# A quarter of w2's last row in twenty-four partitions: an adaLN decode block on one core

## The chip, the cores and the metric

One NeuronCore of a Trainium2 chip runs the whole kernel. The metric is the device time of one execution in microseconds; the median of the runs counts. The engines are called as in the profile: PE is TensorE's matmuls and PEld its weight loads, DVE is VectorE, ACT is ScalarE, POOL is GpSimd, SP is SyncE, which issues nearly all DMAs. A name with a q behind it (SPq, PEq) is the sequencer of that engine.

## What is computed

Two tokens (B = 2, one position each) go through a block with adaptive layer norm. The conditioning vector gives six modulation vectors. Attention runs over the last 4,096 positions of a cache with 8 key-value heads, and a dense feed-forward with SiLU follows. All is float32.

```python
mod = (_silu(c) @ w_mod).reshape(c.shape[0], 6, 1, -1)
sa, ca, ga, sb, cb, gb = (mod[:, 0], mod[:, 1], mod[:, 2], mod[:, 3], mod[:, 4], mod[:, 5])
h = _layernorm(x, axis=-1) * (1 + ca) + sa
x = x + ga * _A_ref(h, A_k_cache, A_v_cache, A_wq, A_wo)   # q = h@wq, softmax(q k) v, @wo
h = _layernorm(x, axis=-1) * (1 + cb) + sb
x = x + gb * _B_ref(h, B_w1, B_w2)                         # silu(h @ w1) @ w2
```

The sizes: D = 512, 32 query heads of 128, F = 1792; w2 has 1,792 rows of 512 columns.

## The kernel before

**The stream.** Every large input passes once through a ring of eight slots of 128 partitions x 16 KB (`slots`, handed out by `stream`). SP issues the loads in the order in which they are written: w_mod, wq, then for each of eight steps a pair of heads of K and of V (`load_pair`, L82, 4 MB each, two slots), wo in two loads, w1 in two, w2 in four (`load_runs`, L93). A load waits until the slots that it takes are free, and so SP runs some loads ahead of the compute. The step's loads are issued in `fetch(s)` (L351): K of step s, then V of step s - 1; `fetch(s + 1)` is called at the beginning of step s.

**The steps.** In step s, DVE transposes K in 32 x 32 blocks (`keys`, L363), PE multiplies it with the queries (`scores`, L376), DVE and ACT build the softmax, and PE multiplies the weights of the step before with V (`weighted`, L450). The queries stand in two constant tiles, `qbd[0]` for the first four heads and `qbd[1]` for the other four (`place`, L316). `scores` of steps 0 to 3 reads `qbd[0]` and that of steps 4 to 7 reads `qbd[1]`.

**How a weight is laid out.** A weight of 1,792 rows is read as 128 partitions of 14 rows, "(p t) e -> p t e": partition p holds rows 14 p to 14 p + 13, and `tile tt` is row tt of every partition, [128, 512]. The hidden vector is brought into the same layout: `uT` [128, 14, 32] holds in column 0 and 16 of its last axis the two tokens, and zeros between them.

**The last product.** w2's four loads are rows 0 to 7 of each partition (2 MB), 8 to 10 (768 KB), 11 and 12 (512 KB), and 13 (256 KB). Each matmul takes a [128, 32] slice of `uT` as weights and writes 32 output rows, chosen by g:

- L663, tiles 0 to 7: the full 512 columns each; tile tt writes rows 32 (tt mod 4) and up of `yw`. `gather` (L548) copies yw to SBUF (L551 on ACT, L552 on DVE) and adds it up into `y` by four matmuls (L554).
- L673, tiles 8 to 10: four matmuls for a tile, g = 0 to 3, 128 columns each, into `y`.
- L688, tiles 11 to 13: for each half h of 64 columns of a block of 128, and for g = 0 to 3, one matmul, into `yl[0]` or `yl[1]`. The last load feeds tile 13, eight of these 24 matmuls.

DVE then forms yp = y * gb + x1 (L696, L697), yo = yl * gb for each half (L701), yo + yp for each half (L704), and SP writes yo out (L706).

**What sets the order.** Instructions wrapped in `inorder` keep their written order on their engine; the others are placed by a scheduler by when their inputs are ready (the copy of L505 stands behind the loop in the code and runs at 31.5 us, before it). `busy(n)` issues n matmuls on data that nobody reads, each into the same 32 rows of `junk` (L567).

Of the kernel before, what the change touches and what calls it, by code (L numbers as in the profile page):

```python
# [10 lines left out]
ALU = mybir.AluOpType  # L11
AX = mybir.AxisListType

P = 128
B, D = 2, 512
HQ, HKV, DH = 32, 8, 128
G = HQ // HKV
F = 1792
EPS = 1e-5
RING = 8  # L20


@with_exitstack
def adaln_block(
# [19 lines left out]
    nc = tc.nc  # L44
# [16 lines left out]
    def const(shape, name):  # L61
        return consts.tile(shape, F32, name=name)

    def bank(tag, name):
        return (psum1 if tag in "CO" else psum).tile([P, 512], F32, tag=tag, name=name)


    slots, turn_of = ring.tile([P, RING, 4096], F32, name="slots"), [0]

    def stream(n=1):  # L70
        i = turn_of[0]
        if n % 2 == 0:
            i += -i % n
        turn_of[0] = i + n
        return slots[:, i % RING : i % RING + n, :].rearrange("p s e -> p (s e)")

    def load_pair(cache, s):


        i, b = divmod(s, B)  # L80
        t = stream(2)
        nc.sync.dma_start(  # L82
            t,
            cache[b, 2 * i : 2 * i + 2, SK - W :, :].rearrange("e (u n) d -> u e (n d)", u=P // 2),
        )
        return t

    def load_runs(w, per, lo, hi):

        e = w.shape[1]  # L90
        n = -(-(hi - lo) * e // 4096)
        t = stream(n)[:, : (hi - lo) * e].rearrange("p (q e) -> p q e", e=e)
        nc.sync.dma_start(t, w.rearrange("(p q) e -> p q e", q=per)[:, lo:hi, :])  # L93
        return t
# [5 lines left out]
    ident = const([P, P], "ident")  # L100
# [6 lines left out]
    for b in range(B):  # L107
# [53 lines left out]
    odd = const([P, 2], "odd")  # L161
    nc.vector.tensor_reduce(
        odd, ident.rearrange("p (a r) -> p r a", r=2), axis=AX.X, op=ALU.add
    )

    selg0, selg = const([P, G], "selg0"), const([P, B, G], "selg")
# [42 lines left out]
    qbd = [const([P, 4, B, 4, 32], f"qbd{n}") for n in range(2)]  # L209
# [11 lines left out]
    def silu_exp(t, name, shape):  # L221

        e = once.tile(shape, F32, tag="silu", name=name)
        nc.vector.tensor_scalar(e, t, -1.0, 87.0, op0=ALU.mult, op1=ALU.min)
        nc.scalar.activation(e, e, AF.Exp)
        nc.vector.tensor_scalar(e, e, 1.0, None, op0=ALU.add)
        nc.vector.reciprocal(e, e)
        return e
# [26 lines left out]
    def turned(t, name):  # L255
        o = const([P, 4, 32], name)
        nc.vector.transpose(o, t.rearrange("p (m k) -> p k m", k=4))  # L257
        return o
# [7 lines left out]
    for k in range(4):  # L266
        ab = wm[:, k, : 2 * D].rearrange("p (s g m) -> p g s m", s=2, g=4)
        cd = wm[:, k, 2 * D :].rearrange("p (s g m) -> p g s m", s=4, g=4)
        for g in range(4):
            r = slice(32 * g, 32 * g + 32)  # L270
            nc.tensor.matmul(m_a[r, :], scT[:, k, :], ab[:, g], start=(k == 0), stop=(k == 3))  # L271
        for g in range(4):
            r = slice(32 * g, 32 * g + 32)
# [19 lines left out]
    hT, uT = const([P, 4, 32], "hT_b"), const([P, F // P, 32], "uT")  # L293
# [6 lines left out]
    for n in range(2):  # L300
        for k in range(4):
            wv = wqt[:, k, :].rearrange("p (n s g m) -> p n g s m", n=2, s=4, g=G)
            for g in range(G):
# [4 lines left out]
                    start=(k == 0),  # L308
                    stop=(k == 3),
                )  # L310

    inorder = tc.keep_in_program_order
# [32 lines left out]


    STEPS = B * HKV // 2
    kt, vt, wot, kT = {}, {}, [], {}
    s_ps, pr, o_ps, o_sb = {}, {}, {}, {}

    def fetch(s):  # L351

        if s < STEPS:
            kt[s] = load_pair(k_cache, s)
        if s > 0:
            vt[s - 1] = load_pair(v_cache, s - 1)

    def keys(s, j):


        kT[s, j] = ktp.tile([P, 64, 32], F32, tag="kT", name=f"kT{s}_{j}")
        for c in range(2):
            inorder(nc.vector.transpose(  # L363
                kT[s, j][:, 32 * c : 32 * c + 32, :],
                kt[s].rearrange("p (n j r) -> p j n r", j=4, r=32)[:, j, 32 * c : 32 * c + 32, :],
            ))

    def scores(s, j):

        if j == 0:  # L370
            s_ps[s] = bank("A", f"s{s}")
        i, b = divmod(s, B)
        for c in range(2):
            for e in range(2):
                r, h = 64 * e + 32 * c, 2 * i + e
                inorder(nc.tensor.matmul(  # L376
                    s_ps[s][r : r + 32, :],
                    qbd[h // 4][:, h % 4, b, j, :],
                    kT[s, j][:, 32 * c : 32 * c + 32, e:32:2],
                    start=(j == 0),  # L380
                    stop=(j == 3),
                ))
# [34 lines left out]
    def turn(s):  # L417

        xp = once.tile([P, 16, 32], F32, tag="xp", name=f"xp{s}")
        inorder(nc.vector.transpose(xp, pr[s]))  # L420
        zp = once.tile([P, 4, 16, 16], F32, tag="zp", name=f"zp{s}")
        inorder(nc.vector.tensor_mul(  # L422
            zp,
            xp[:, None, :, 0:16].to_broadcast([P, 4, 16, 16]),
            quarter[:, :, None, None].to_broadcast([P, 4, 16, 16]),
        ))
        tp = bank("C", f"pT{s}")[:, : 2 * P]
        for i in range(4):
            inorder(nc.tensor.matmul(  # L429
                tp[32 * i : 32 * i + 32, :],  # L430
                mix.rearrange("p v e -> p (v e)"),
                zp.rearrange("p y t x -> p (y t) x")[:, :, 4 * i : 4 * i + 4],
                start=True,
                stop=True,
            ))
        for e in range(2):
            inorder(nc.scalar.activation(  # L437
                ptb[s % 2][:, :, e, :],
                tp.rearrange("p (w z) -> p w z", z=16),
                AF.Copy,  # L440
                scale=odd[:, e : e + 1],
            ))
# [19 lines left out]
    def collect(s):  # L462
# [3 lines left out]
        for m in range(4):  # L466
# [5 lines left out]
                start=(s == 0 and m < 2),  # L472
                stop=(s == STEPS - 1 and m >= 2),
                skip_group_check=True,
            ))

    fetch(0)
    keys(0, 0)
    for s in range(STEPS + 1):
        if s < STEPS:  # L480
            fetch(s + 1)
            scores(s, 0)
        if s > 0 and s != STEPS - 1:
            turn(s - 1)
        if s > 1:
            collect(s - 2)
        if s == 2:
            place(1)
        if s < STEPS:
            for j in range(1, 4):  # L490
# [15 lines left out]
    ax = once.tile([P, P], F32, tag="ax", name="ax")  # L506
    for lo, hi in ((0, 24), (24, 32)):
        wt = load_runs(wo, 32, lo, hi)
        wot.extend(wt[:, q, :] for q in range(hi - lo))
    xT = turned(x_sp, "xT")  # L510
    w1t = []
    for lo, hi in ((0, 3), (3, 4)):
# [11 lines left out]
    for r in (0, 64):  # L524
# [4 lines left out]
            start=True,  # L529
            stop=True,  # L530
# [33 lines left out]
    def busy(n):  # L564

        for _ in range(n):
            inorder(nc.tensor.matmul(  # L567
                junk[0:32, :],
                id4,
                quad.rearrange("p m y -> p (m y)"),  # L570
                start=True,
                stop=True,
            ))
# [5 lines left out]
    for q in range(28):  # L579
        g = q % 4  # L580
# [4 lines left out]
            start=(q < 4),  # L585
            stop=(q >= 24),
        ))
    for q in range(28, 32):
        for g in range(4):
# [4 lines left out]
                start=(q == 28),  # L594
                stop=False,
            ))
    gather(ao, acc, "acc_o_sb", False, True)
    busy(1)
    T2, WIDE = F // P, 8
    w2t = {}  # L600
    for lo, hi in ((0, WIDE), (WIDE, 11), (11, 13), (13, T2)):
        wt = load_runs(w2, T2, lo, hi)
        for tt in range(lo, hi):
            w2t[tt] = wt[:, tt - lo, :]
    aoT = once.tile([P, 4, 32], F32, tag="zp", name="aoT")
    nc.vector.transpose(aoT, ao.rearrange("p (m k) -> p k m", k=4))
    x1T = once.tile([P, 4, B], F32, tag="x1T", name="x1T")
# [19 lines left out]
    for k in range(4):  # L627
        for g in range(4):
# [4 lines left out]
                start=(k == 0),  # L633
                stop=(k == 3),
# [22 lines left out]
        )  # L657
    sg = silu_exp(z, "sgh", [P, T2, B])
    nc.vector.tensor_mul(uT[:, :, 0:32:16], z, sg)
    yw = bank("D", "acc_yw")  # L660
    for tt in range(WIDE):
        g = tt % 4
        inorder(nc.tensor.matmul(  # L663
            yw[32 * g : 32 * g + 32, :],
            uT[:, tt, :],
            w2t[tt],
            start=(tt < 4),
            stop=(tt >= WIDE - 4),
        ))
    y = bank("D", "acc_y")[:, :P]  # L670
    for tt in range(WIDE, 11):
        for g in range(4):
# [4 lines left out]
                start=(tt == WIDE),  # L677
                stop=False,
# [2 lines left out]

    H = P // 2
    yl = [bank("A", f"acc_l{h}")[:, :H] for h in range(2)]
    for tt in range(11, T2):
        for h in range(2):
            for g in range(4):
                lo = g * P + h * H
                inorder(nc.tensor.matmul(  # L688
                    yl[h][32 * g : 32 * g + 32, :],
                    uT[:, tt, :],  # L690
                    w2t[tt][:, lo : lo + H],
                    start=(tt == 11),
                    stop=(tt == T2 - 1),
                ))
    yp = once.tile([P, P], F32, tag="xp", name="yp")
    inorder(nc.vector.tensor_mul(yp, y, gb))  # L696
    inorder(nc.vector.tensor_add(yp, yp, x1))  # L697
# [1 line left out]
    for h in range(2):  # L699
        r = slice(h * H, (h + 1) * H)  # L700
        inorder(nc.vector.tensor_mul(yo[:, r], yl[h], gb[:, r]))  # L701
    for h in range(2):
        r = slice(h * H, (h + 1) * H)
# [30 lines left out]
```

## Time and profile before

| | |
|---|---|
| median of 3 runs | 235.45 us (235.43 to 235.75) |
| span of the profiled execution, first to last instruction | 233.7 us |
| busy in it: PE / PEld / DVE / ACT / POOL | 160.2 / 43.1 / 115.6 / 28.5 / 10.6 us |
| mean granted clock of PE | 0.934 of full speed, 1.00 from 190 us on |
| DMA | 3,795 packets, 97.68 MB |
| chain that ended last | DMA 60%, issue 17%, DVE 14%, PE 6% of the span |

The page of the profile gives busy times over the whole span; the chain of waits follows back what released each step, and the timeline lists instructions with their start in us, their length, and in brackets how long the engine had been idle before them and what ended that. x16 means sixteen instructions merged into one line. fp32 matmuls appear as two passes, so eight matmuls are x16. The length of a matmul is modelled and includes its way through the array; starts are as recorded.

### The profile page before, as it was taken

To read this page: it belongs to the slowest core of one execution; us is meant where nothing else is said; L and a number is where in the kernel's file an instruction comes from. 1 tells how busy PE (TensorE), PEld (TensorE's weight loads), DVE (VectorE), ACT (ScalarE), POOL (GpSimd) and SP (SyncE) were. 2 spreads that over 40 slices of the span, in tenths; PEclk is the share of its full clock that TensorE was granted. 3 is DMA by queue.
4 is the path that set the end of the run, shared out by engine and by line. 5 is a ranking of instruction groups with operands and counts; after the bars stand their busy time and mean duration, and the time that the engine had idled before them with its cause. 6 is when DMAs were issued, how large, how long until landed. Compare 5 with 4: busy or idle time off the path is not lost.

```text
span 233.7 us, 2571 instructions
## 1 busy us (share of the span) xinstructions
PE 160.2 (69%) x1070; PEld 43.1 (18%) x1070; DVE 115.6 (49%) x179; ACT 28.5 (12%) x64; POOL 10.6 (5%) x35
## 2 busy tenths in 40 slices
PE   0005916959577839787689759758769777869784
PEld 0001401211111111221111202201112122314223
DVE  3004140178795758696197189249559540101232
ACT  1100210000311120120210201111030031002020
POOL 8600010000000000000000000000000000000000
PEclk9999975879979997999979988999997999999999
DMA  7998998999999999999999999999999999989991
GB/s 269 446 520 381 426 471 359 440 443 428 415 421 449 440 443 421 421 423 449 443 437 426 415 429 449 437 437 429 404 444 443 437 423 471 446 362 427 423 412 57
DMA packets 3795, 97.68 MB, mean 418 GB/s; under 512 B 433, under 2 KB 457, under 8 KB 969
## 3 DMA queue, kind: packets, MB, share of 16 engines
q1 hardware_dynamic: 3768, 97.53, 97.2%
q8 instruction: 8, 0.13, 0.2%
q14 instruction: 3, 0.02, 0.0%
q10 hardware_dynamic: 16, 0.00, 0.0%
HBM read 97.53 MB, written 0.00 MB: 417 GB/s over the span
## 4 chain that ended last, share of the span: by engine, by line
DMA 60%; issue 17%; DVE 14%; PE 6%; POOL 1%; POOLq 0%; SPq 0%; ACT 0%; DVEq 0%
DMA slots<-in_A_k_cache_dram 22%; DMA slots<-in_A_wq_dram 14%; DMA slots<-in_B_w_dram 12%; DMA slots<-in_A_v_cache_dram 12%; DVE kT L363 11%; PE q L304 3%; PE o L450 2%; DVE zp L422 1%; PE acc_yw L663 1%; DVE xp L420 1%; PE acc_y L673 0%; DVE xc L102 0%; POOL qg L321 0%; DVE qT L317 0%; PE acc_y L554 0%
## 5 line engine op out<-in xcount | busy, mean ns | idle before, releaser
L363 DVE STREAM_TRANSPOSE kT<-slots 128x1024 f32<-128x1024 f32 x64 | 73.7, 1210 | 22.9 <-DMA slots<-in_A_k_cache_dram 22.8
L376 PE MATMUL s<-kT,qbd 128*32 128x512 f32 x256 | 68.5, 703 | 17.9 <-DVE kT L363 17.0
L450 PE MATMUL o<-slots,ptb 128*32 128x512 f32 x256 | 29.1, 595 | 2.2 <-DMA slots<-in_A_v_cache_dram 2.2
L376 PEld LDWEIGHTS s<-kT,qbd 128*32 128x32 f32 x256 | 9.8, 113 | 66.9 <-DVE kT L363 62.9
L271 PE MATMUL m_a<-slots,scT 128*32 128x256 f32 x32 | 4.4, 507 | 20.4 <-DVE scT L263 20.4
L304 PE MATMUL q<-slots,hq_T 128*32 128x512 f32 x64 | 9.7, 773 | 7.4 <-DMA slots<-in_A_wq_dram 7.4
L450 PEld LDWEIGHTS o<-slots,ptb 128*32 128x32 f32 x256 | 7.7, 109 | 16.7 <-issue 16.6
L406 ACT COPY bias<-bp 128x1 f32<-128x1 f32 x8 | 1.3, 159 | 75.8 <-PE bp L404 75.8
L386 DVE TENSOR_REDUCE mx<-s 128x1 f32<-128x512 f32 x8 | 5.5, 691 | 9.6 <-PE s L376 9.6
L567 PE MATMUL junk<-quad,id 128*32 128x512 f32 x22 | 10.2, 596 | 0.0
L437 ACT ACTIVATE ptb<-pT,odd 128x256 f32<-128x256 f32 x16 | 6.7, 472 | 26.0 <-PE pT L429 26.0
L422 DVE TENSOR_TENSOR zp<-xp,quarter 128x1024 f32<-128x1024 f32 x8 | 9.8, 1225 | 0.2
L429 PE MATMUL pT<-zp,mix 128*32 128x256 f32 x64 | 5.8, 438 | 4.0 <-DVE zp L422 4.0
L317 DVE STREAM_TRANSPOSE qT<-q 128x512 f32<-128x512 f32 x2 | 1.4, 717 | 13.5 <-PE q L304 12.0
L581 PE MATMUL acc_o<-slots,oTn 128*32 128x512 f32 x56 | 6.2, 593 | 2.3 <-DMA slots<-in_A_wo_dram 2.3
L460 ACT COPY ob<-o 128x512 f32<-128x512 f32 x8 | 4.7, 586 | 24.4 <-PE o L450 24.4
L552 DVE COPY acc_o_sb<-acc_o 128x256 f32<-128x256 f32 x1 | 0.4, 425 | 14.1 <-ACT acc_o_sb L551 14.1
L388 PE MATMUL mT<-ident,mx 128*1 128x128 f32 x16 | 3.0, 270 | 6.3 <-DVE mx L386 6.3
L420 DVE STREAM_TRANSPOSE xp<-pr 128x512 f32<-128x512 f32 x8 | 5.5, 685 | 3.4 <-ACT pr L408 3.4
L257 DVE STREAM_TRANSPOSE cT<-xc 128x128 f32<-128x128 f32 x1 | 0.4, 401 | 13.7 <-DMA xc<-in_c_dram 13.7
L274 PE MATMUL m_sp<-slots,scT 128*32 128x512 f32 x32 | 7.2, 730 | 0.0
L468 PE MATMUL o_all<-ob,selh 128*64 128x128 f32 x64 | 5.9, 313 | 0.8 <-ACT ob L460 0.8
(140 smaller groups left out, 93.7 us busy)
## 6 DMA issues: line engine op xcount, KB each, us to landing
slots<-in_A_k_cache_dram SPq DMA_DIRECT2D x8, 4096.0 KB, 27.6
slots<-in_A_v_cache_dram SPq DMA_DIRECT2D x8, 4096.0 KB, 27.7
slots<-in_w_mod_dram SPq DMA_DIRECT2D x1, 6144.0 KB, 17.2
slots<-in_A_wo_dram SPq DMA_DIRECT2D x1, 6144.0 KB
slots<-in_B_w_dram SPq DMA_DIRECT2D x1, 2688.0 KB
slots<-in_A_wo_dram SPq DMA_DIRECT2D x1, 2048.0 KB, 29.5
slots<-in_B_w_dram SPq DMA_DIRECT2D x1, 2048.0 KB
slots<-in_B_w_dram SPq DMA_DIRECT2D x1, 896.0 KB
```

The lines of the kernel that those rows point to most:

```text
L274: nc.tensor.matmul(m_sp[r, :], scT[:, k, :], cd[:, g], start=(k == 0), stop=(k == 3))
L304: nc.tensor.matmul(q_ps[n][32 * g : 32 * g + 32, :], hq_T[:, k, :], wv[:, n, g], start=(k == 0), stop=(k == 3),)
L363: inorder(nc.vector.transpose(kT[s, j][:, 32 * c : 32 * c + 32, :], kt[s].rearrange("p (n j r) -> p j n r", j=4, r=32)[:, j, 32 * c : 32 * ...
L376: inorder(nc.tensor.matmul(s_ps[s][r : r + 32, :], qbd[h // 4][:, h % 4, b, j, :], kT[s, j][:, 32 * c : 32 * c + 32, e:32:2], start=(j == ...
L420: inorder(nc.vector.transpose(xp, pr[s]))
L422: inorder(nc.vector.tensor_mul(zp, xp[:, None, :, 0:16].to_broadcast([P, 4, 16, 16]), quarter[:, :, None, None].to_broadcast([P, 4, 16, 16 ...
L429: inorder(nc.tensor.matmul(tp[32 * i : 32 * i + 32, :], mix.rearrange("p v e -> p (v e)"), zp.rearrange("p y t x -> p (y t) x")[:, :, 4 * ...
L437: inorder(nc.scalar.activation(ptb[s % 2][:, :, e, :], tp.rearrange("p (w z) -> p w z", z=16), AF.Copy, scale=odd[:, e : e + 1],))
L450: inorder(nc.tensor.matmul(o_ps[s][r : r + 32, :], ptb[s % 2][:, w].rearrange("p e z -> p (e z)"), vt[s].rearrange("p (c w m f d) -> p c f ...
L468: inorder(nc.tensor.matmul(o_all[r : r + 64, :], selh[:, m, lo : lo + 2 * HQ], o_sb[s][:, m * DH : (m + 1) * DH], start=(s == 0 and m < 2) ...
L567: inorder(nc.tensor.matmul(junk[0:32, :], id4, quad.rearrange("p m y -> p (m y)"), start=True, stop=True,))
L581: inorder(nc.tensor.matmul(acc[32 * g : 32 * g + 32, :], oTn[:, q, :], wot[q], start=(q < 4), stop=(q >= 24),))
```

## The change

Of tile 13 of w2 (row 13 of each partition) the columns 384 to 511, those of g = 3, are no longer loaded with the rest for partitions 8 to 127. These 120 pieces of 128 columns go to 24 partitions, five side by side in each (`far` [48, 5, 128], rows 0 to 11 and 32 to 43), inside the memory of `qbd[0]`. Eight loads (`move`) of 3 x 5 pieces bring them: in the order of issue behind V of step 4, K of 6, V of 5, K of 7, V of 6 and V of 7, and one behind each of the two loads of wo. Partitions 0 to 7 (`own` = 8) get their 128 columns by a load of their own, and the other 384 columns of the row come for all partitions in one load.

The hidden values of those 120 partitions must stand in the same 24 partitions. `uj` multiplies tile 13 of `uT` with `slot`, which marks at which of the five places a partition's piece stands; the matmul `up` with the selection matrix `away` sends them to the 24 rows; a copy puts them into `uF` [48, 5, 32], zeroed before. In L688's place the columns of g = 3 are then made by six matmuls for each half: five of 48 rows with `uF` and `far`, one of 8 rows with `uT` and `own`'s columns. They stand between tile 12 and the matmuls of g = 0 to 2 of tile 13.

```diff
+NE, NR, NJ = 3, 4, 5
...
+    own = P - 2 * NR * NJ * NE
+    away, slot = const([P, 48], "away"), const([P, NJ], "slot")
+    nc.gpsimd.memset(away, 0.0)
+    for h in range(2):
+        nc.vector.tensor_reduce(
+            away[:, 32 * h : 32 * h + NE * NR].rearrange("p (e r) -> p e r", e=NE),
+            ident[:, own + 60 * h : own + 60 * h + 60].rearrange(
+                "p (r j e) -> p e r j", r=NR, j=NJ
+            ),
+            axis=AX.X,
+            op=ALU.add,
+        )
+    nc.vector.tensor_reduce(
+        slot,
+        ident[:, own:].rearrange("p (hr j e) -> p j hr e", j=NJ, e=NE),
+        axis=AX.XY,
+        op=ALU.add,
+    )
...
+    T2, WIDE = F // P, 8
+    w2p = w2.rearrange("(p t) e -> p t e", t=T2)
+    spare = qbd[0].rearrange("p s b j c -> p (s b j c)")
+    far = spare[:, : NJ * P].rearrange("p (j m) -> p j m", j=NJ)
+    uF = spare[:, NJ * P : NJ * (P + 32)].rearrange("p (j n) -> p j n", j=NJ)
+    uj = spare[:, NJ * (P + 32) : NJ * (P + 32 + B)].rearrange("p (j b) -> p j b", j=NJ)
+    moves = [(h, r) for h in range(2) for r in range(NR)]
+
+    def move():
+
+        h, r = moves.pop(0)
+        lo = own + 60 * h + NJ * NE * r
+        nc.sync.dma_start(
+            far[32 * h : 32 * h + NE * NR].rearrange("(e r) j m -> e r j m", r=NR)[:, r],
+            w2p[lo : lo + NJ * NE, T2 - 1, D - P :].rearrange("(j e) m -> e j m", e=NE),
+        )
...
             kt[s] = load_pair(k_cache, s)
+            if s > STEPS // 2 + 1:
+                move()
         if s > 0:
             vt[s - 1] = load_pair(v_cache, s - 1)
+            if s > STEPS // 2:
+                move()
...
         wt = load_runs(wo, 32, lo, hi)
+        move()
         wot.extend(wt[:, q, :] for q in range(hi - lo))
+    nc.gpsimd.memset(uF, 0.0)
...
-    for lo, hi in ((0, WIDE), (WIDE, 11), (11, 13), (13, T2)):
+    for lo, hi in ((0, WIDE), (WIDE, 11), (11, 13)):
...
+    w2l = stream(1)[:, :D]
+    nc.sync.dma_start(w2l[0:own, D - P :], w2p[0:own, T2 - 1, D - P :])
+    nc.sync.dma_start(w2l[:, : D - P], w2p[:, T2 - 1, : D - P])
...
     nc.vector.tensor_mul(uT[:, :, 0:32:16], z, sg)
+    nc.vector.tensor_mul(
+        uj,
+        uT[:, T2 - 1, 0:32:16][:, None, :].to_broadcast([P, NJ, B]),
+        slot[:, :, None].to_broadcast([P, NJ, B]),
+    )
     yw = bank("D", "acc_yw")
...
+    up = bank("C", "up")[:48, : NJ * B]
+    inorder(nc.tensor.matmul(
+        up, away, uj.rearrange("p j b -> p (j b)"), start=True, stop=True
+    ))
+    nc.vector.tensor_copy(uF[:48, :, 0:32:16], up.rearrange("p (j b) -> p j b", b=B))
     y = bank("D", "acc_y")[:, :P]
...
-    for tt in range(11, T2):
+    def last(h, g, lhs, rhs, start=False, stop=False):
+        inorder(nc.tensor.matmul(
+            yl[h][32 * g : 32 * g + 32, :], lhs, rhs, start=start, stop=stop
+        ))
+
+    for tt in range(11, T2 - 1):
         for h in range(2):
             for g in range(4):
                 lo = g * P + h * H
-                inorder(nc.tensor.matmul(
-                    yl[h][32 * g : 32 * g + 32, :],
-                    uT[:, tt, :],
-                    w2t[tt][:, lo : lo + H],
-                    start=(tt == 11),
-                    stop=(tt == T2 - 1),
-                ))
+                last(h, g, uT[:, tt, :], w2t[tt][:, lo : lo + H], start=(tt == 11))
+    for h in range(2):
+        for j in range(NJ):
+            last(h, 3, uF[:48, j, :], far[:48, j, h * H : h * H + H])
+        last(
+            h, 3, uT[0:own, T2 - 1, :], w2l[0:own, 3 * P + h * H : 3 * P + h * H + H], stop=True
+        )
+    for h in range(2):
+        for g in range(3):
+            lo = g * P + h * H
+            last(h, g, uT[:, T2 - 1, :], w2l[:, lo : lo + H], stop=True)
```

More of the change, by code (lines that the diff above doesn't have):

```diff
@@ L598, in adaln_block @@
     busy(1)
-    T2, WIDE = F // P, 8
     w2t = {}
-    for lo, hi in ((0, WIDE), (WIDE, 11), (11, 13), (13, T2)):
+    for lo, hi in ((0, WIDE), (WIDE, 11), (11, 13)):
         wt = load_runs(w2, T2, lo, hi)
```

## The prediction

> **What bounds the kernel now.** I read the page first, then the chain of waits that ended last, then the last three microseconds of the timeline.
>
> ```profile
> span 233.7 us, 2571 instructions
> DMA  7998998999999999999999999999999999989991
> DMA packets 3795, 97.68 MB, mean 418 GB/s; under 512 B 433, under 2 KB 457, under 8 KB 969
> ```
>
> The DMA engines are full from the second of the 40 slices to the last but one: the kernel streams 97.68 MB at 418 GB/s, 26 GB/s for each of 16 engines. What can be gained in the stream is what the last bytes cost; what can be lost is anything behind them. The end of the chain, in order of time (start, duration):
>
> ```profile
> 197.41 28.93 DMA slots<-in_B_w_dram
> 226.34 0.14 issue
> 226.47 1.92 PE acc_yw L663 x16
> 228.40 0.78 PE acc_y L673 x24
> 229.18 0.20 PE acc_y L554 x4
> ...
> 229.39 0.44 PE acc_y L554 x4
> ...
> 229.85 0.30 DVE yp L696
> ...
> 230.18 0.29 DVE yp L697
> 230.47 0.35 DVE yo L701 x2
> 230.82 0.13 DVE yo L704
> ```
>
> The end hangs on the first of the four loads of w2 (rows 0 to 7 of a partition, landed at 226.34), not on the last one. From there PE and DVE work through to yo. The change shortens the last load alone, so I look at where that one stands. The first two rows are DMA issues (KB each, us from issue to landing), the third is the line that issues, the fourth is from the timeline:
>
> ```profile
> slots<-in_A_k_cache_dram SPq DMA_DIRECT2D x8, 4096.0 KB, 27.6
> slots<-in_B_w_dram SPq DMA_DIRECT2D x1, 256.0 KB, 17.3
> L93 SPq DMA_DIRECT2D slots<-in_B_w_dram x6: 328/328/328, 190.2 to 212.7; - x6
> 229.54 0.97 PE L688 MATMUL acc_l<-slots,uT 128*32 128x64 f32 x47
> L688 PE MATMUL acc_l<-slots,uT x48: 216/219/243, 229.5 to 230.3; 128*32 128x64 f32 x48
> ```
>
> Issued at 212.7, the last load lands 17.3 later, at 230.0. L688 works off tiles 11, 12 and 13 with 16 matmuls each (8 in the code, two passes for each). They start (0.97 - 0.219) / 46 = 0.016 us apart, so tile 13's turn comes at 229.54 + 32 x 0.016 = 230.05: PE arrives just as the load lands. And L701 starts at 230.47, when L697 is done, so DVE's own chain ends with them. Three things tie: an earlier landing alone can bring no more than about 0.05 us.
>
> **The transfers.** 120 partitions give up 512 of the 2,048 bytes of their last row. Its 128 rows are eight for each of 16 engines, so it loses 4 KB on each, at 26 GB/s 0.16 us. By the tie above 0.05 of it can count, and only if PE is ready then. The 61 KB come back as 120 pieces behind eight earlier loads. The load's outer size is 3; if three engines carry it all, each takes 40 pieces, 20 KB, at 26 GB/s 0.79 us at least. Whether that shows depends on the engines' lead (stretch, length, busy time of PE, PEld, DVE, ACT, POOL, clock, DMA share, GB/s):
>
> ```profile
> 226.00:227.00 1.00, 0.53 (x8) 0.28 (x12) 0.00 (x0) 0.00 (x0) 0.00 (x0) 1.00 1.03 430
> 228.25:228.50 0.25, 0.25 (x12) 0.21 (x12) 0.00 (x0) 0.00 (x0) 0.00 (x0) 1.00 0.54 221
> 228.75:229.00 0.25, 0.25 (x17) 0.23 (x11) 0.09 (x1) 0.13 (x1) 0.00 (x0) 1.00 0.49 188
> 229.50:229.75 0.25, 0.25 (x17) 0.25 (x19) 0.00 (x0) 0.00 (x0) 0.00 (x0) 1.00 0.05 16
> q8 instruction: 8, 0.13, 0.2%
> ```
>
> All engines work at 226 to 227; from 228.25 half of them do; at 229.5 none. So half have a lead of about 1.2 us. The instruction row is one likely reason: 8 packets of 16 KB took 0.2% of 16 engines' 233.7 us, some 0.9 us each, on one engine at a time. If the three engines are of the early half, 0.79 us vanishes in the lead: cost 0 here, and +0.3 to +0.8 otherwise (rival B). The Trainium skill, page "DMA: Bandwidth & Descriptors", section "Why a DMA increments its semaphore by 16 and not by 1", says that such a load is split over the largest number of engines up to 16 that divides both outer sizes, and takes the lowest-numbered: three here. No row shows engine numbers; were the pieces spread over all 16, the sum would be the same, as the landing does not count.
>
> **SP, POOL and DVE.** These rows price what is added and show its cover:
>
> ```profile
> L82 SPq DMA_DIRECT2D slots<-in_A_k_cache_dram x8: 534/534/605, 28.7 to 146.6; - x8
> SPq L82 <- DVE kT L363: 76.8, 7, 13.7
> 17.78 0.40 DVE L257 STREAM_TRANSPOSE cT<-xc 128x128 f32<-128x128 f32 x1 [13.68 <-DMA xc<-in_c_dram]
> 30.69 0.53 POOL L289 TENSOR_SCALAR mod_sp<-mod_sp 128x128 f32<-128x128 f32 x1 [21.22 <-ACT mod_sp L288]
> L162 DVE TENSOR_REDUCE odd<-ident 128x2 f32<-128x128 f32 x1 | 0.3, 274 | 0.0
> 228.91 0.42 DVE L552 COPY acc_y_sb<-acc_yw 128x256 f32<-128x256 f32 x1 [3.39 <-ACT acc_y_sb L551]
> ```
>
> Nine more issues on SP (eight moves, and the last load becomes two) cost about 0.53 each; SP sits waiting for 76.8 us on DVE alone, and a K load issued 27.6 us ahead of its landing needs 4 MB / 418 GB/s = 10.0 us of the stream, so 0.5 us later is nothing. The moves write into qbd[0], last read by step 3's scores; the load ahead of the first move (V of step 4) already waits for step 2's L450, which stands behind those scores on PE. Even if each move had to wait for the piece before it to land, the next load would be issued about one load (10 us) ahead of its turn instead of two or three. The reductions for away and slot (three of 0.27) fall into DVE's idle 13.68 us ahead of L257, the memsets into POOL's 21.22. The product uj falls into DVE's 3.39 ahead of L552. Without these covers they would cost some 0.3 us apiece. All cost 0.
>
> **The matmul `up` and the copy of uF.** `up` goes between L663 and L673. There is a row for such an insertion, L638 within L629:
>
> ```profile
> 219.43 1.71 PE L629 MATMUL hid<-slots,hT_b 128*32 128x448 f32 x16 [0.94 <-DMA slots<-in_B_w_dram]
> 221.07 0.38 PE L638 MATMUL var_b<-vs,mean 128*128 128x2 f32 x2
> 221.39 1.71 PE L629 MATMUL hid<-slots,hT_b 128*32 128x448 f32 x16
> 221.79 0.13 PEld L629 LDWEIGHTS hid<-slots,hT_b 128*32 128x32 f32 x4 [0.25 <-issue]
> 222.16 0.13 PEld L629 LDWEIGHTS hid<-slots,hT_b 128*32 128x32 f32 x4 [0.25 <-issue]
> L638 PE MATMUL var_b<-vs,mean 128*128 128x2 f32 x2 | 0.4, 262 | 0.0
> ```
>
> A round of four L629 matmuls takes 222.16 - 221.79 = 0.37, so the second sixteen would start at 219.43 + 4 x 0.37 = 220.91; they start at 221.39. The insertion cost 0.48: 0.38 - 0.26 = 0.12 between its two passes, and 0.36 for two changes of the array's shape (128*32 to 128*128 and back), 0.18 each. `up` costs PE at most that. L673 then ends late, but the second half of L554 starts at 229.39, only when DVE's L552 (228.91 + 0.42) is done. So about 0.2 us of it are covered, and the copy of uF fits ahead of 228.91 if `up` is done by 228.7. I take +0.05, between 0 and +0.3.
>
> **The matmuls of the moved columns.** Tile 13's two matmuls for g = 3 become twelve (five pieces and `own`, for two halves), 24 passes, all into the same 32 output rows. Today g runs through four row groups. What rotation is worth is in two more rows:
>
> ```profile
> L567 PE MATMUL junk<-quad,id 128*32 128x512 f32 x12 | 5.3, 594 | 0.0
> L541 PE MATMUL oq<-on,quad 128*128 128x64 f32 x8 | 1.1, 277 | 0.8 <-DVE on L538 0.8
> ```
>
> L567 writes one row group over and over: (5.3 - 0.594) / 11 = 0.43 for 512 columns. L663, of the same shape, rotates: 1.92 us for 16, some 0.1 each. So one group is four times slower than four; for 64 columns 0.43 / 8 = 0.054. Bounds: 0.016, L688's rotating pace, and (1.1 - 0.277) / 7 = 0.118 of L541, 64 columns into one output with four times wider weights. I take 0.054, the same width of weights and one group: 24 x 0.054 = **1.30 us**, and nothing hides it, since PE reaches it at 230.05 with all else done. It also falls behind the landing, whose gain is thereby lost.
>
> These matmuls differ in rows too: 128 (tile 12), 48 (pieces), 8 (own), 48, 8, and 128 again for g = 0 to 2: five changes of shape. A change cost 0.18 at L638, there with weights four times as wide; no row shows one of rows alone. Bounds 0 and 0.18, I take 0.12: **+0.60**. The Trainium skill, "TensorEngine Tiling (Array Packing)", section "Key Properties", says that a change of tiling mode drains the engine, while different tiles run in parallel; the L638 row agrees. By that rule all five count, and without it the sum would be 0.60 less.
>
> Removed: four passes at 0.016 and PE's small wait, together 0.1; 0.05 is DVE's slack. **Sum**: 1.30 + 0.60 + 0.05 - 0.10 - 0.05 = +1.80. The profiled execution spans 233.7, and the median of the runs, 235.45, is 1.75 above that, which the change does not touch; so 235.45 + 1.80 = 237.25, **237.2 us**. Both unknown prices at their bounds, one at a time: pace 0.016 gives 236.3 and 0.118 gives 238.8; changes of shape at 0 and 0.18 give 236.6 and 237.5.
>
> **The rivals.** A, not slower: the pieces stream abreast. If PE issues the twelve as fast as the rotating ones and a change of rows alone drains nothing, 24 x 0.016 = 0.38, less 0.15, plus 0.05: +0.3, 235.7. It decides under 0.023 a matmul, where the sum falls under 0.2%. For it: L688's own pace; against it: L567. B, an engine of the late half: one of the three lags; then every load from step 5 on, w2's first too, lands up to 0.8 later. From the lag inside the late half I take +0.5 on top: 237.7. For it: half of the engines are late. C, the wide price: the twelve run at L541's pace, 238.8; its weights speak against it. D, SP: a move holds a load back until the stream runs dry. Against it stands the lead of 10 us: only a wait as long as SP's longest on DVE, 13.7, would use it up, and the stream would stand for 3.7 us: 240.9.
>
> **How the numbers follow.** Forecast 0.60, A 0.06, B 0.20, C 0.08, D 0.03; 0.03 is left, 0.02 of it for a gain that I do not see. The likeliest case alone reaches from 236.6 to 237.5. The range, 236.1 to 238.8, takes in the bounds of the two prices, B and C, and leaves out A and D. Under 0.2% (0.47 us) a measurement here can't be told from no change: faster 0.02, within 0.2% 0.06, slower 0.92.
>
> **What would show it.** In the changed profile: L663's wait ends at 226.3 as before (B: later); the last load lands some 0.1 to 0.2 earlier; the g = 3 matmuls begin near 230.1 and take about 1.9 us with gaps at each change of rows; DVE waits for PE ahead of L701, where today it waits for nothing. If L701 starts before 230.9, or the chain ends in a DMA, the prediction is wrong.

## The result and the profile after

The changed kernel takes 237.94 us (median of 4 runs, 237.79 to 238.09), the kernel before beside it 235.60 (235.43 to 235.76): a ratio of 1.0099, 95% interval 1.0085 to 1.0113, or 2.34 us more. The profiled execution of the changed kernel is the one of 237.79 us. Its page:

```profile
span 235.6 us, 2638 instructions
DMA packets 3955, 97.69 MB, mean 415 GB/s; under 512 B 464, under 2 KB 744, under 8 KB 1128
```

There are 160 packets more, as many bytes as before, and the span is 1.9 us longer. The lines have moved: L663 is now L713, L673 is L728, L554 is L597, L688 is L740, L696 and L697 are L760 and L761, L701 is L765, L704 is L768; `up` is L721. The chain that ended last in the changed kernel (start, duration), in order of time:

```profile
198.98 27.28 DMA slots<-in_B_w_dram
226.26 0.14 issue
226.39 1.92 PE acc_yw L713 x16
228.32 0.19 PE up L721 x2
228.50 0.79 PE acc_y L728 x24
229.30 0.38 PE acc_y L597 x7
229.68 2.57 PE acc_l L740 x61
232.24 0.02 issue
232.27 0.36 DVE yo L765 x2
```

It starts with the same load, which landed at 226.26 (226.34 before), and the first 3.3 us have hardly changed. But it no longer runs over to DVE's yp: PE stays in it with L740 until 232.24, and yo starts at 232.27, 1.80 later than before (230.47). The timeline shows what PE does there (start, length, form of the instructions, and in brackets what DVE waited for):

```profile
228.25 0.26 PE L721 MATMUL up<-qbd,away 128*48 128x10 f32 x2
229.46 0.71 PE L740 MATMUL acc_l<-slots,uT 128*32 128x64 f32 x32
229.78 0.29 DVE L760 TENSOR_TENSOR yp<-acc_y,mod_sp 128x128 f32<-128x128 f32 x1 [0.52 <-PE acc_y L597]
230.10 0.74 PE L740 MATMUL acc_l<-qbd 48*32 48x64 f32 x10
230.78 0.29 PE L740 MATMUL acc_l<-slots,uT 8*32 8x64 f32 x2
231.00 0.74 PE L740 MATMUL acc_l<-qbd 48*32 48x64 f32 x10
231.67 0.65 PE L740 MATMUL acc_l<-slots,uT 8*32 8x64 f32 x14
232.27 0.36 DVE L765 TENSOR_TENSOR yo<-acc_l,mod_sp 128x64 f32<-128x64 f32 x2 [1.87 <-PE acc_l L740]
```

The view of L740 alone has the min, median and max ns of one of these matmuls:

```profile
L740 PE MATMUL acc_l<-qbd x20: 216/216/240, 230.1 to 231.5; 48*32 48x64 f32 x20
```

Tiles 11 and 12 are the 32 passes at 229.46, at 0.016 each. The moved columns begin at 230.10. The ten passes on pieces take 0.74 us and the last of them 0.216, so their starts lie (0.74 - 0.216) / 9 = 0.058 apart on average; in the trace it is 0.056, with one step of 0.080 behind the change of shape ahead of them. From 230.10 to 231.00 lie twelve passes and two changes of shape: 0.90 - 12 x 0.056 = 0.23, or **0.11 for a change**. The merged group at 231.67 is `own`'s two passes and the twelve of g = 0 to 2. DVE, which waited for nothing ahead of L701 before, now waits 1.87 us for PE.

The last load in the changed kernel's timeline of SP, and its row among the DMA issues (KB, us to landing):

```profile
213.82 0.36 SPq L649 DMA_DIRECT2D slots<-in_B_w_dram  x1
```

```profile
slots<-in_B_w_dram SPq DMA_DIRECT2D x1, 192.0 KB, 16.0
```

It lands at 213.82 + 16.0 = 229.8, 0.2 earlier than before, and nobody waits for it. The windows of the changed kernel, in the columns of the prediction:

```profile
228.25:228.50 0.25, 0.25 (x10) 0.23 (x10) 0.00 (x0) 0.07 (x1) 0.00 (x0) 1.00 0.70 279
228.75:229.00 0.25, 0.25 (x17) 0.25 (x12) 0.19 (x2) 0.05 (x1) 0.00 (x0) 1.00 0.52 193
229.50:229.75 0.25, 0.25 (x24) 0.25 (x23) 0.00 (x0) 0.00 (x0) 0.00 (x0) 1.00 0.00 0
```

At 228.25 a share of 0.70 of the DMA engines still works, against 0.54 before: (0.70 - 0.54) x 16 = 2.6, some three engines more. By 228.75 the share is back near a half.

The trace also keeps the times at which a DMA raises the semaphore of a load: sixteen times when a load of 128 partitions lands, read here as once for each engine, and three times when a move lands. For w2's first load in the kernel before, eight of the sixteen come within 0.56 us of the first, and the other eight 1.38 to 2.03 us behind it. In the changed kernel five come within 0.27 us, three 1.16 to 1.28 behind the first, and eight 1.54 to 1.89. So three engines that used to be done early carry the moves and lose about 1 us by them, and they still end ahead of the late ones.

### The profile page after: what moved, and what is told of

Read it like the earlier page. It is cut to its first block, busy times and chain, and to the rows that moved or that the text cites. A ratio compares the mean times of both kernels' runs of the same rounds, so it can differ in the third digit from the quotient of the medians.

```text
span 235.6 us, 2638 instructions
## 1 busy us (share of the span) xinstructions
PE 164.4 (70%) x1092; PEld 44.7 (19%) x1092; DVE 116.4 (49%) x184; ACT 28.5 (12%) x64; POOL 10.8 (5%) x37
## 4 chain that ended last, share of the span: by engine, by line
DMA 60%; PE 18%; DVE 17%; ACT 2%; issue 1%; ACTq 0%; POOL 0%; DVEq 0%; POOLq 0%
DMA slots<-in_A_k_cache_dram 43%; DVE kT L404 12%; DMA slots<-in_B_w_dram 12%; PE s L417 7%; DMA xc<-in_c_dram 6%; PE o L491 4%; PE m_sp L294 2%; DVE zp L463 2%; DVE xp L461 1%; PE acc_l L740 1%; PE m_a L291 1%; PE acc_yw L713 1%; ACT pr L449 1%; DVE mx L427 1%; ACT L449 1%
## 5 line engine op out<-in xcount | busy, mean ns | idle before, releaser
L417 PE MATMUL s<-kT,qbd 128*32 128x512 f32 x256 | 69.6, 684 | 18.7 <-DVE kT L404 17.5
L491 PE MATMUL o<-slots,ptb 128*32 128x512 f32 x256 | 30.5, 619 | 0.1
L324 PE MATMUL q<-slots,hq_T 128*32 128x512 f32 x64 | 9.1, 731 | 7.8 <-DMA slots<-in_A_wq_dram 7.8
L610 PE MATMUL junk<-quad,id 128*32 128x512 f32 x22 | 11.6, 666 | 0.0
L624 PE MATMUL acc_o<-slots,oTn 128*32 128x512 f32 x56 | 7.0, 593 | 0.0
L294 PE MATMUL m_sp<-slots,scT 128*32 128x512 f32 x32 | 6.6, 712 | 0.0
```

Of the source, the lines that this page charges most:

```text
L294: nc.tensor.matmul(m_sp[r, :], scT[:, k, :], cd[:, g], start=(k == 0), stop=(k == 3))
L324: nc.tensor.matmul(q_ps[n][32 * g : 32 * g + 32, :], hq_T[:, k, :], wv[:, n, g], start=(k == 0), stop=(k == 3),)
L417: inorder(nc.tensor.matmul(s_ps[s][r : r + 32, :], qbd[h // 4][:, h % 4, b, j, :], kT[s, j][:, 32 * c : 32 * c + 32, e:32:2], start=(j == ...
L491: inorder(nc.tensor.matmul(o_ps[s][r : r + 32, :], ptb[s % 2][:, w].rearrange("p e z -> p (e z)"), vt[s].rearrange("p (c w m f d) -> p c f ...
L610: inorder(nc.tensor.matmul(junk[0:32, :], id4, quad.rearrange("p m y -> p (m y)"), start=True, stop=True,))
L624: inorder(nc.tensor.matmul(acc[32 * g : 32 * g + 32, :], oTn[:, q, :], wot[q], start=(q < 4), stop=(q >= 24),))
```

## The experiments

All times are medians, each beside runs of the kernel before on the same chip. "Outside" is the median of a run's time less its span. "Tail" is, in the profiled execution, the time from the first matmul on w2 (L663, now L713) to the start of yo (L701, now L765); it leaves out when w2 landed. For the changed kernel it is 232.27 - 226.39 = 5.88.

| kernel | time, us | against before, 95% interval | median span | outside | tail |
|---|---|---|---|---|---|
| before (beside the first four) | 235.53 | | 233.7 | 1.79 | 4.00 |
| the change | 237.94 | 1.0085 to 1.0113 | 235.9 | 2.12 | 5.88 |
| moves and `up`, old tail | 235.75 | 1.0002 to 1.0020 | 233.6 | 2.14 | 4.00 |
| no moves | 237.70 | 1.0082 to 1.0110 | 235.65 | 2.05 | 5.87 |
| all rows | 237.07 | 1.0055 to 1.0083 | 235.0 | 2.10 | 5.21 |
| rotated | 237.11 | 1.0056 to 1.0083 | 235.05 | 2.04 | 5.20 |
| rotated, all rows | 236.19 | 1.0017 to 1.0040 | 234.1 | 2.08 | 4.33 |
| every move twice, old tail | 236.74 | 1.0037 to 1.0066 | 234.7 | 2.05 | 4.04 |
| constants alone | 235.67 | 0.9990 to 1.0009 | 233.8 | 1.81 | 4.00 |

**The old tail with everything else kept.** The moves, `uj`, `up` and the copy of uF stay; the last load and its matmuls are those of before.

```diff
-    for lo, hi in ((0, WIDE), (WIDE, 11), (11, 13)):
+    for lo, hi in ((0, WIDE), (WIDE, 11), (11, 13), (13, T2)):
...
-    for tt in range(11, T2 - 1):
+    for tt in range(11, T2):
...
-    for h in range(2):
-        for j in range(NJ):
-            last(h, 3, uF[:48, j, :], far[:48, j, h * H : h * H + H])
...
```

> The eight moves, the matmul up and the copy of uF stay, but the last load and the last matmuls are those of before (all 128 columns of g = 3 come with the last load; the moved pieces are loaded and not read). Theory, the cost is PE's serial tail alone: within 0.1 us of before, the first load of w2 lands at 226.3 +- 0.1, DVE is again free of PE ahead of yo. Rival, the small loads or the three engines cost it: +1 us or more, with the first load of w2 landing that much later.

235.75 against 235.53. The end of its chain:

```profile
226.58 1.92 PE acc_yw L710 x16
228.51 0.19 PE up L718 x2
...
230.29 0.29 DVE yp L749
230.58 0.35 DVE yo L753 x2
```

The tail is 230.58 - 226.58 = 4.00, that of before to the hundredth, and the span (233.6 in the median) is no longer than before (233.7). `up` takes 0.19 in the chain and costs nothing at its end, as DVE's yp sets it. So the eight moves, their issues, `up` and the copy cost nothing inside the span; what is left, 0.2 us, lies outside it (below).

**The change without its moves.** No `move()`; a memset zeroes `far`, so the moved pieces' share is missing from the result.

```diff
-            if s > STEPS // 2 + 1:
-                move()
...
-            if s > STEPS // 2:
-                move()
...
-        move()
...
-    nc.gpsimd.memset(uF, 0.0)
+    nc.gpsimd.memset(spare[:, : NJ * (P + 32)], 0.0)
```

> No piece is moved (far is set to zero, so 120 partitions' share of the 128 columns is left out of the result); the last matmuls stay as changed. Theory of the serial tail: as slow as the changed kernel, within 0.1 us, the tail from the first matmul of 48 rows to the last of tile 13 again 2.0 us. Rival, the moves cost it: about 235.6.

237.70, or 2.17 more than before, though 61 KB fewer are read. The end of its chain, with a tail of 232.19 - 226.32 = 5.87:

```profile
226.32 1.92 PE acc_yw L708 x16
...
229.64 2.53 PE acc_l L735 x59
232.17 0.02 issue
232.19 0.35 DVE yo L760 x2
```

Read with the run before it, the two halves fall cleanly apart: transfers alone, no longer a span; matmuls alone, all of it.

**No changes of shape.** The matmuls of the moved columns take all 128 rows: the rows that hold no piece meet zeros in uF, and `own`'s one takes uT's tile 13 with all but the first eight partitions masked to zero.

```diff
+    uO, first = spare[:, 810:842], spare[:, 842:843]
+    nc.vector.tensor_reduce(first, ident[:, :own], axis=AX.X, op=ALU.add)
+    nc.vector.tensor_mul(uO, uT[:, T2 - 1, :], first.to_broadcast([P, 32]))
...
-            last(h, 3, uF[:48, j, :], far[:48, j, h * H : h * H + H])
+            last(h, 3, uF[:, j, :], far[:, j, h * H : h * H + H])
         last(
-            h, 3, uT[0:own, T2 - 1, :], w2l[0:own, 3 * P + h * H : 3 * P + h * H + H], stop=True
+            h, 3, uO, w2l[:, 3 * P + h * H : 3 * P + h * H + H], stop=True
         )
```

> The matmuls of the moved columns take all 128 rows (weights zero in the unused rows), so the shape of the array no longer changes within the tail; twenty-four passes stay in one row group. Theory, five changes at 0.11 us each (the starts in the changed kernel's trace are 0.144 apart at a change and 0.080 behind it, 0.056 elsewhere): 0.55 us faster than the changed kernel, 237.4. Rival, fewer rows are cheaper or the drain is part of the matmuls' own length: within 0.1 us of the changed kernel.

237.07. Its timeline, the first ten passes and three lines from the end of the moved columns:

```profile
230.12 0.72 PE L743 MATMUL acc_l<-qbd 128*32 128x64 f32 x10
...
231.24 0.26 PE L743 MATMUL acc_l<-slots,uT 128*32 128x64 f32 x3
231.29 0.22 PE L743 MATMUL acc_l<-qbd 128*32 128x64 f32 x1
...
231.41 0.22 PE L743 MATMUL acc_l<-slots,qbd 128*32 128x64 f32 x1
```

and two steps of its chain:

```profile
226.50 1.92 PE acc_yw L713 x16
...
231.71 0.36 DVE yo L768 x2
```

The ten passes still take 0.72: with 128 rows or 48, one row group of the output is as slow. But the tail falls from 5.88 to 5.21, by 0.67 for five changes of shape, or 0.13 each. Of this, 5 x 0.114 = 0.57 is what the starts show at the changes. The other 0.10 is read here as overlap: the first passes of g = 0 to 2 (`slots,uT`, 231.24) now start 0.16 ahead of `own`'s last pass (`slots,qbd`, 231.41), where in the changed kernel a change of shape held them until 0.14 behind it.

**Rotated.** The pieces' matmuls go round the four row groups; the changes of shape stay.

```diff
-            last(h, 3, uF[:48, j, :], far[:48, j, h * H : h * H + H])
+            last(h, (3 + j) % 4, uF[:48, j, :], far[:48, j, h * H : h * H + H])
```

> The five pieces of a half go to row groups 3, 0, 1, 2, 3 in turn (their sums land in other columns, so the result's last columns are wrong); rows, shapes and count stay. Theory, one row group is what makes them serial: a half's ten passes take 4 x 0.056 = 0.22 us in place of 0.56, twice 0.34 = 0.6 to 0.7 us faster than the changed kernel, 237.3. Rival, the pace is set by the weight loads of 48 rows or by issue: no change.

237.11. Its timeline:

```profile
230.04 0.41 PE L740 MATMUL acc_l<-qbd 48*32 48x64 f32 x10
230.60 0.41 PE L740 MATMUL acc_l<-qbd 48*32 48x64 f32 x10
```

and its chain:

```profile
226.33 1.92 PE acc_yw L713 x16
...
231.53 0.35 DVE yo L765 x2
```

Ten passes now take 0.41 in place of 0.74. Nothing but the row group of the output has changed, so that alone is the reason for the pace of 0.056: twice 0.33 is 0.66, and the tail loses 5.88 - 5.20 = 0.68. The recorded starts of L688 in the kernel before show how rotation helps. Four passes, one for each row group, start from 230.157 to 230.177, and the next four from 230.213 to 230.233, again 0.056 behind. One row group takes a pass every 0.056 us, and four of them side by side make that about 0.016 a pass.

**Both.** All rows and rotated, `own`'s matmul in group 0. The edit is shown against the kernel with all rows.

```diff
-            last(h, 3, uF[:, j, :], far[:, j, h * H : h * H + H])
+            last(h, (3 + j) % 4, uF[:, j, :], far[:, j, h * H : h * H + H], stop=(j == 4))
         last(
-            h, 3, uO, w2l[:, 3 * P + h * H : 3 * P + h * H + H], stop=True
+            h, 0, uO, w2l[:, 3 * P + h * H : 3 * P + h * H + H]
         )
```

> Both edits at once: all 128 rows, and pieces and own in row groups 3, 0, 1, 2, 3, 0 in turn (the sums land in other columns, so the result's last columns are wrong). Theory, the two terms add: no change of shape (0.56 less) and four passes of 0.056 a group and half in place of twelve (2 x 8 x 0.056 = 0.90 less): 1.4 to 1.5 us faster than the changed kernel, 236.3, some 0.8 over before for the matmuls that are more. Rival, the terms overlap (a drain hidden in the serial stream): 236.8 or more.

236.19. The end of its chain:

```profile
226.36 1.92 PE acc_yw L713 x16
...
229.67 1.00 PE acc_l L743 x60
230.67 0.02 issue
230.69 0.36 DVE yo L768 x2
```

The tail is 4.33, so 1.55 of the 1.88 are gone: 0.67 + 0.68 = 1.35 by the two runs alone. The other 0.20 was not measured apart; `own`'s four passes, which now rotate too, would make 4 x 0.040 = 0.16 of it by the paces. What remains over before, 0.33, agrees with 20 more passes at 0.016 (24 less the four removed): 0.32. So nearly all of the tail's extra time is accounted for.

**Every move twice.** The old tail as above, and each move issued a second time. It was meant to measure how much lead the three engines have.

```diff
-        nc.sync.dma_start(
+        for _ in range(2):
+          nc.sync.dma_start(
```

> The kernel with the old tail, every one of the eight moves issued twice. Theory, the three engines had a lead of 1.2 us or more and one dose (40 pieces, about 1.0 us on each) just fits: with a second dose of 1.0 us they end last, the first load of w2 lands 0.5 to 1.0 us later than with one dose, and the time rises by as much, to 236.2 to 236.8. Rival, the pieces cost the stream nothing (spread over all engines, or run beside the loads): 235.8 as with one dose.

236.74, inside what was expected for a lead that one dose uses up, and w2's first matmul starts at 227.51, not 226.58. But the profile gives another reason. In the view of waits, SP's longest entry (total, times, longest):

```profile
SPq L381 <- DMA qbd<-in_B_w_dram: 71.7, 8, 16.2
```

The second copy writes the same bytes as the first, so SP waits each time until the first has landed, behind the big loads ahead of it. Its issues in the timeline, w1's first load last, and then the same load in the changed kernel, the first of a group of three:

```profile
209.01 1.50 SPq L381 DMA_DIRECT2D qbd<-in_B_w_dram  x2
210.61 0.35 SPq L94 DMA_DIRECT2D slots<-in_B_w_dram  x1
```

```profile
193.84 5.47 SPq L94 DMA_DIRECT2D slots<-in_B_w_dram  x3
```

It comes 16.8 us later, and the stream runs thin. The window from 212 to 214, with every move twice and then in the changed kernel (share and GB/s at the end):

```profile
212.00:214.00 2.00, 2.00 (x24) 0.69 (x20) 0.00 (x0) 0.00 (x0) 0.00 (x0) 1.00 0.79 314
```

```profile
212.00:214.00 2.00, 2.00 (x24) 0.70 (x17) 0.00 (x0) 0.00 (x0) 0.00 (x0) 1.00 0.97 407
```
The landing times say something of the lead as well. The second load of wo landed over 2.07 us with one dose (the run with the old tail). Here it lands over 2.89 us, with one engine 0.84 us behind all others. So with a second dose one engine ends behind the late half. How much of the 0.93 comes from that, and how much from the thin stream, is not separated: the test is **inconclusive** on the size of the lead. What it does show is the price of rival D where it is real: a small load that waits on SP uses up the 10 us by which the queue is ahead.

**Using the lead without new matmuls.** If engines finish unevenly, giving the early ones more of an ordinary load might help the kernel before. Its second load of w1 (128 partitions of 7 KB) was cut along the partitions in five ways, with nothing else changed.

```diff
+        cuts = [0, 112, 115, 118, 121, 124, 127, 128]
+        for a, b in zip(cuts, cuts[1:]):
+            nc.sync.dma_start(t[a:b], src[a:b])
...
-        wt = load_runs(w1, 4, lo, hi)
+        wt = load_runs(w1, 4, lo, hi) if lo == 0 else load_split(w1, 4, lo, hi)
```

> The kernel before, with the lead of the first three engines used without any matmul: the second load of w1 is split into one of 112 partitions (7 in place of 8 rows of 7 KB on each engine) and five of 3 partitions and one of 1, which the theory puts on the first three engines. Theory: every other engine has 7 KB less, at 26 GB/s 0.27 us, the first load of w2 lands 0.2 to 0.3 earlier, and the time falls by as much, to 235.3. Rival, the three engines' 36 to 43 KB more (1.4 to 1.6 us) is over their lead, or the six small loads hold SP: same or up to 0.5 us slower.

The others have the cuts 112 + 4 x 4, 112 + 2 x 8, 64 + 64, and 112 + 16:

> The kernel before with the second load of w1 cut into 112 partitions and four loads of four, so that, if four partitions go to four engines, these four carry 11 rows of 7 KB where they carried 8, and the other twelve 7. Theory (some engines had a lead of 1.2 us, and late ones set the landing): w2's first load lands 7 KB earlier on the late engines, at 26 GB/s 0.27 us, at 226.1, and the end follows: 235.2 us, ratio 0.999. Rival 1 (the lowest four are not all early, or have less lead than 0.8): 235.5 to 236.1. Rival 2 (what slowed the cut into seven was not the eight semaphores but the narrow loads themselves, whose packets took twice their time): w1's first load lands after 220 and the end is above 236.5.

> As the run beside it, cut into 112 partitions and two loads of eight: if eight partitions go to eight engines, these carry 9 rows and the other eight 7. Theory: the late ones gain 0.27 us, the early ones lose as much of 1.2: 235.2 us. Rival 1 (early and late engines do not fall into the lower and upper eight, so that late ones get more): 235.7. Rival 2 (narrow loads slow the packets around them): above 236.5, with w1's first load landing after 220.

> The kernel before with the second load of w1 cut into two of 64 partitions: four rows of 7 KB for each of 16 engines and load, no engine gets more than another, one issue more. If it is the narrow loads (to fewer than 16 engines) that slowed the cuts into seven, five and three: as before, 235.6, with 410 to 440 GB/s from 218 to 222. If any cut of this load does it: above 238, with some 200 GB/s there. If it is a step of 7 rows instead of 8 from engine to engine: as before.

> Cut into 112 and 16 partitions: seven rows and one row for each of 16 engines, again no engine with more than another. If the narrow loads slowed it: 235.6. If any cut does it, or the step of 7 rows from engine to engine: above 238, with some 200 GB/s from 218 to 222; the run beside it tells these two apart.

| cut | time, us | against before, 95% interval |
|---|---|---|
| 112 + 5 x 3 + 1 | 238.28 | 1.0107 to 1.0150 |
| 112 + 4 x 4 | 239.58 | 1.0147 to 1.0175 |
| 112 + 2 x 8 | 239.21 | 1.0132 to 1.0160 |
| 64 + 64 | 238.78 | 1.0119 to 1.0153 |
| 112 + 16 | 239.02 | 1.0130 to 1.0168 |

None brought a gain. The first is slower than both its expectation and its rival; in the other four the rival that named a slow stream came out. In the timeline of the first, SP issued w2's first load only at 221.41, where it was 197.41 before:

```profile
196.48 16.83 SPq L104 DMA_DIRECT2D slots<-in_B_w_dram  x7
221.41 3.73 SPq L93 DMA_DIRECT2D slots<-in_B_w_dram  x4
```

SP waited there for w1's first load, which landed at 221.34: the large loads take turns with eight semaphores in the trace, these two have the same one, and seven pieces in place of one load moved w2 to it. That looked like the cause. With five pieces w2 still waits, until 208.17, but with three or two it is issued at 197.4 to 198.8, and the stream slows all the same. One window in three kernels, the one before, 64 + 64, and 112 + 16, and the step of w2's first load in the chain of the last:

```profile
218.00:220.00 2.00, 1.06 (x10) 0.34 (x12) 0.16 (x1) 0.00 (x0) 0.00 (x0) 1.00 0.97 411
```

```profile
218.00:220.00 2.00, 1.45 (x5) 0.43 (x4) 1.35 (x10) 0.00 (x0) 0.00 (x0) 1.00 0.94 219
```

```profile
218.00:220.00 2.00, 0.77 (x2) 0.00 (x0) 0.41 (x3) 0.00 (x0) 0.00 (x0) 1.00 0.97 211
```

```profile
197.66 32.69 DMA slots<-in_B_w_dram
```

The engines are as busy as before but move half the bytes; with 112 + 16, w2's first load, issued at 197.66 as before, takes 32.69 us in place of 28.93. Two equal halves, which give no engine more than another, do it too, so neither narrow loads nor uneven shares are the reason. That each half covers only 64 partitions can't be the whole reason either, since 112 are as slow. All five cuts go along the partitions. w2 comes in four loads that each cover all 128 partitions, and the stream runs at 430 GB/s there (226 to 227 in the prediction's windows). A cut of this load that leaves all 128 partitions in each piece was not tried. Why a cut along the partitions halves the pace is open, and so is whether the lead could be used in some other way.

**The constants alone.** Every kernel with the change's code has 2.04 to 2.14 us outside its span, every one without it 1.7 to 1.8. The kernel before was given `away` and `slot`, which nobody reads there.

```diff
+    away, slot = const([P, 48], "away"), const([P, NJ], "slot")
+    nc.gpsimd.memset(away, 0.0)
...
+    nc.vector.tensor_reduce(
+        slot,
...
```

> The kernel before with the constants of the change alone (away and slot: one memset on POOL, three reductions on DVE), which nobody reads. The span should stay at 233.7. The question is the time outside the span, 1.8 us in the kernel before and 2.05 to 2.2 in every kernel that has these constants, up and uF. If the constants (code at the beginning of the program) make it: 235.8, with 2.05 outside the span. If it is the matmul up, the product uj or the copy of uF near the end: 235.55, with 1.8.

235.67, with 1.81 outside: it is not the constants. What is common to all kernels with the longer time is the memset on POOL in the middle (of uF, or of uF and `far`), `uj`, `up` and the copy; which of them adds the 0.3 was not tried.

## Why the prediction came out as it did

The mechanism was right, and most prices were close.

- **The passes into one row group**: predicted 0.054 each from L567, measured 0.056; 24 make 1.34 for 1.30. The rotated kernel shows the cause directly.
- **The changes of shape**: predicted 0.12 each, measured 0.11 by the starts, and 0.13 by taking them away, overlap included. The Trainium skill, "TensorEngine Tiling (Array Packing)", section "Key Properties", has a change of tiling mode drain the engine and different tiles run in parallel. Both halves show here, and a change of rows alone (128 to 48 to 8) counts as one.
- **`up`**: predicted +0.05, measured 0. It takes 0.19 of PE, and yp starts as long after w2's landing as before: 229.78 - 226.26 = 3.52 against 229.85 - 226.34 = 3.51.
- **The transfers, SP, POOL and DVE** at nothing: right inside the span. The last load landed 0.2 earlier and gained nothing, as PE was far behind. The prediction's readings of the lead hold: three engines carry the moves, and none is later than the late half. One cover was misread: uF lies in `qbd[0]`, so its memset can't run in POOL's 21.22 us at the start. It ran at 109.02, where POOL had been idle for 24.60, and cost nothing either.
- **Why half of the engines are late**: the prediction named the instruction packets as a likely reason, and the landing times of the kernel before bear it out. By 58 us, behind the first packet (41.8), two engines land more than 1.1 us after the first to land. Behind each further packet it is one more: three at 87 us (a packet starts at 79.1), four at 106 (104.5), five at 145 (134.7), six at 174 (163.4), seven at 193 (191.5), and eight at 219 (212.3). With every move twice, where the stream ran thin, fourteen of sixteen land within 0.5 us at 220. That a packet sets one engine back until the stream pauses is inferred from this; no run left the packets out.
- **The sum at yo**: +1.80 predicted, +1.80 measured. The agreement to the hundredth is luck. Counted from w2's first matmul the tail grew by 1.88; that this matmul started 0.08 earlier (226.39 against 226.47) was not in the sum. The measured passes and changes make 1.34 + 0.57 = 1.91, and only 0.03 came off it, where the prediction took off 0.15 for the removed passes, PE's wait and DVE's slack. `up`, 0.05 too dear, made up for a part.
- **What was mis-sized** is the sentence that the 1.75 us outside the span are untouched, for which it showed no row. The prediction was 237.2; the runs' median is 237.94. Outside is 2.12 in the median, about 0.3 to 0.4 more, in every kernel that holds the new code, even with the old tail. The rest is the spread of the span (235.6 in the profiled run, 235.9 in the other three).

The rivals. A, the pieces streaming abreast, fell: they do so only when rotated. B, a late engine, fell: w2 landed at 226.26, not later. C fell: the pace was 0.056, not 0.118. D fell for the change, whose moves wait for no piece before them, but the kernel with every move twice shows how it comes about. The signs named are all there: L713's wait ends near 226.3, the last load lands 0.2 earlier, the moved columns start at 230.10 and take 1.8 us with gaps, and DVE waits ahead of yo.

## What to carry to other kernels

Before bytes are taken off the last load, look which of the things that end together is really last: here a load that landed 0.2 earlier was worth nothing, while matmuls put behind it cost their full time. Price a new matmul by a row that writes where it will write: passes of 64 columns cost 0.056 into one row group of the output and 0.016 over four, and each change of rows between them 0.11, or 0.13 with the overlap that it prevents. When a small kernel tail is summed, compare the time outside the span as well, since a change can add some tenths there that no row shows.

## What was not expected of the hardware

- Cutting one load of 128 partitions into two halves of 64 partitions, in the middle of a full stream, halved the stream's pace there (219 GB/s at a share of 0.94, 411 at 0.97 uncut) and cost 3.2 us; eight small loads of 512-byte pieces, in the changed kernel, cost nothing in the span.
- The time outside the span changes with the kernel's code: 1.7 to 1.8 us without the change's code, 2.04 to 2.14 with it.
- Under a stream that never pauses, the engines drift apart one by one: all sixteen land within 0.6 us of each other at 37 us, and eight of them 1.38 us or more behind the first at 226.
